# FFT mixer with two MLPs on one core: conversion slots, the centring of w1b, the start of the transforms and the banks of the transposes moved

## The chip, the core and the metric

The kernel runs on one core of a Trainium2 chip. The metric is the device time of one execution in microseconds (us). Work is spread over TensorE (PE, matmuls and transposes), VectorE (DVE), ScalarE (ACT), GpSimd (POOL) and the queue of SyncE (SP), which issues most DMAs. Each engine works through its own instructions in order, and semaphores make it wait for the others.

## What is computed

For four sequences of 3136 tokens with 256 channels, in float32:

```python
y = irfft(rfft(x, axis=1) * (filt_r + 1j * filt_i), n=3136)     # per channel
u = y + (y.transpose(0, 2, 1) @ U @ V).transpose(0, 2, 1)       # U 3136x32, V 32x3136
x2 = u + relu(u @ w1) @ w2                                      # 256 -> 1024 -> 256
xn = (x2 - mean(x2)) / sqrt(var(x2) + 1e-6) * g                 # over the channels
out = x2 + relu(xn @ w1b) @ w2b                                 # 256 -> 1024 -> 256
```

U, V and the four weights arrive as 64-bit floats.

## The kernel before

**Precision.** A float32 operand is split into a high and a low half (`hh`/`hl`, `ah`/`al`, `w1h`/`w1l` ...), and a product is made of three matmuls (high by high, high by low, low by high) at the fast rate.

**Main loop.** The 12544 tokens are cut into 25 blocks of 512. Phase ("a", k) is the first MLP of block k, ("b", k) the second. A phase has eight steps, one for each 128 of the 1024 hidden columns f. Step idx issues the first-layer matmuls of its f (`m1`, L671, into a bank `psh` from the pool `ps_h` of three), and the second-layer matmuls of the step two before (`m2`, L690 to L699, into `pso` from the pool `ps_o` of four). ACT makes `hh` from `psh`, then DVE makes `hl`. The steps begin with a0 f 0 to 3, a1 f 0 to 3, a0 f 4 to 7, a1 f 4 to 7 (steps 0 to 15), then a2 (16 to 23), b0, b1, a3, b2, a4, b3, a5 (from step 72). So the `m2` of a0 with f = 6 stands in step 12, and b0 begins in step 24. `end` closes a phase: for an a phase it spreads residual sums, halves and transposes on DVE over the steps behind it, for a b phase it scales and stores the output (`x2t`, L733).

**Units.** 28 units of 448 tokens hold the result of the inverse transform's last stage. `load_unit` loads `wt` of a unit from `bd` in DRAM (SP, L634), `unit` makes `ah` and `al` from it (PE, L642 and L644). Seven units make a batch, and unit 7 is the first of batch 1. It can only be loaded once the transform of batch 1 has ended with `tk` (`tstk`), and it is emitted in step 75 (f = 3 of a5, which looks ahead to block 6 by `ahead`).

**Transforms.** Batch 0 is transformed by `First` ahead of the main loop, batches 1 to 3 by the generator `fft` beside it. In each main step after `FFT0` a credit grows by `RATE` (by 0.4 once batch 1 is done), and each whole credit pulls the generator once. A batch takes 36 pulls: 1 for the first loads, 15 for stage one (L200 to L202 and `ze`), 2 empty, 17 for stage two, the filter and the way back (`be`, stored to `bd`), 1 for `tk`.

**First.** `rows` (eight rows, j = 0 to 7) does stage one of batch 0: PE multiplies `x` by `c` into `pz` (L450), DVE and ACT copy one half each to `big`. `c` is spread from a table of half size by two DVE operations (`spread`, L413), two rows ahead. `columns` (17 steps j) does the rest: PE turns a piece of `big` into `psz` (L538, bank "t", the only one of its pool), ACT copies it to `z`, PE transforms `z` (`ps2`, L555), ACT crosses it over (`psx`) and DVE and POOL apply the filter (`ya`, `xs`; `hl`, `hh` on odd turns; L228 to L232). Three steps later PE transforms back (`ps3`, L564, two banks of `ps_o`). In the step after that the "spill" copies it to `big` again (ACT for dh = 0, DVE for dh = 1), and DVE adds up the projection (`d`, L526 and L528).

**Conversions.** A weight is converted from 64 bits by a job of `to32`: ACT starts it with two operations (L808, L809), four word operations on DVE follow (L795 to L801), POOL multiplies and adds (L813, L815), `keep` makes the high half and `last` the low half. `stagger` runs 18 jobs; each `next(pr)` is one slot. Job i starts in slot 4 i, makes one word operation in each of the next four slots, is kept in slot 4 i + 8 and ends in slot 4 i + 9. The rows take slots 0 to 11 (`ROWSLOTS`), the columns one slot in each of steps 0 to 11 (`COLSLOTS`, slots 12 to 23), and each main step takes two, so step idx has slots 24 + 2 idx and 25 + 2 idx. Job 9 makes `w2h` and `w2l` for f = 6, 7; jobs 10, 11, 13 and 14 make `w1b`. Both jobs of one half of `w1b` are scaled by g (`wg`, L876), and behind the second one `after` is filled with the steps of the centring, one for each slot: `less` (PE sums the columns with four matmuls, L895, and DVE subtracts, L897), `high` (ACT), `low` twice (POOL, L904). `u_parts` (step 10) puts one more operation on POOL, `uh_sb` (L491).

**Order.** The program is recorded in the order in which it is written (`tc.manual_schedule`), and each engine keeps that order. A tile of a pool waits until the tile that had its buffer was read for the last time.

Of the kernel before, what the change touches and what calls it, by code (L numbers as in the profile page):

```python
# [10 lines left out]
F32 = mybir.dt.float32  # L11
# [3 lines left out]
AF = mybir.ActivationFunctionType  # L15
ALU = mybir.AluOpType
# [3 lines left out]
NB, N, D, R, FF = 4, 3136, 256, 32, 1024  # L20
P = 128
PP, NM, NG = 112, 28, 28
# [15 lines left out]
SLOTS, UAHEAD = 8, 2  # L38
PACE = 4
ROWSLOTS = (1, 2, 2, 2, 3, 3, 3, 4, 5, 5, 6, 6)  # L40
COLSLOTS = tuple(range(12))
VSTEP = 11
DIRECT = 4

PARTS, UPARTS = (0, 1, 2, 5, 6, 8), 10
LEAD = 3
FFT0, RATE = 25, 0.75

XTURN, XREAD, XSTAT, XROOT = (3, 4), 8, (10, 11), 12
BW = 32  # L50
# [90 lines left out]
def fft_mixer_kernel(ctx: ExitStack, tc: tile.TileContext, x, U, V, flt, w1, w2, gln, w1b, w2b,  # L141
                     c_fwd32, c_d32, c_e32, c_fwd, c_inv, c_e, c_d, c_w, out):
    nc = tc.nc
# [6 lines left out]
    ps_o = ctx.enter_context(tc.tile_pool(name="ps_o", bufs=4, space=PSUM))  # L150
    ps_t = ctx.enter_context(tc.tile_pool(name="ps_t", bufs=1, space=PSUM))
# [15 lines left out]
    def acopy(o, i, scale=1.0):  # L167
        nc.scalar.activation(out=o, in_=i, func=AF.Copy, scale=scale)  # L168
# [26 lines left out]
    def wide(dt, tag, name, w, bufs=2):  # L195
        t = fp.tile([PP, 2 * (D + R)], dt, tag=tag, name=name, bufs=bufs)
        return t[:, :2 * w].rearrange("p (a d) -> p a d", a=2)
# [6 lines left out]
    def flat(t):  # L204
        return t.rearrange("p a d -> p (a d)")
# [166 lines left out]
    class First:  # L372
# [36 lines left out]
        def spread(self, j):  # L409

            if j < NM // 4:
                for i in range(2):
                    nc.vector.tensor_scalar(out=self.c[j][:, :, i::2], in0=self.half[j // 2][:, j % 2 * 4:j % 2 * 4 + 4],  # L413
                                            scalar1=w_sb[:PP, 2 + i:3 + i], scalar2=None, op0=ALU.mult)

        def u32(self):
            hs, ls, ts = ([fp.tile([P, 512], F32, tag=tag, name=f"u{tag}", bufs=2)[:PP, :448] for j in range(2)]
# [82 lines left out]
        def columns(self):  # L500


            sp = Spectrum(0, self.flt)
            zt, n, w = {}, NCH, PP + R
            d0, d1 = self.d
            self.t = d1[:, 1, 0:KT * 2 * R].rearrange("p (h g r) -> p h g r", h=KT, g=2)
            turns = [self.u_half(h) for h in (1, 0)]

            def slot(g):
                return d1[:, 0] if g == 0 else d0[:, g % SLOTS]  # L510

            def total(j):
                if ADDL <= j < n + ADDL:
                    cross = sp.y[n - 1 - j + ADDL][1]
                    if cross:
                        cross()

            def spill(pvs, i):
                for dh, pv in enumerate(pvs):
                    (nc.vector.tensor_copy if dh else acopy)(self.big[:, dh, 2 * i * PP:2 * (i + 1) * PP].rearrange("p (g w) -> p g w", w=PP), pv[:, :, :PP])  # L520

            def project(pvs, i):
                for dh, pv in enumerate(pvs):
                    acc = self.t[:, dh]
                    if i == n - 1:
                        nc.vector.tensor_copy(acc, pv[:, :, PP:])  # L526
                    else:
                        nc.vector.tensor_tensor(out=acc, in0=pv[:, :, PP:], in1=acc, op=ALU.add)  # L528

            due = None  # L530
            for j in range(n + BACKL):
                if j < n:
                    i = n - 1 - j
                    ps = ps_t.tile([P, 512], F32, tag="t", name="psz")
                    for g in range(2):
                        for dh in range(KT):
                            a = g * D + dh * P
                            nc.tensor.transpose(ps[:PP, a:a + P], self.big[:, dh, (2 * i + g) * PP:(2 * i + g + 1) * PP], ident)  # L538
                total(j)
                if due:  # L540
                    spill(*due)
                    project(*due)
                due = None
                if j < n:
                    zt[i] = wide(F32, "fin", "z0", D, 3)
                    acopy(flat(zt[i]), ps[:PP])
                if 0 < j <= n:
                    i = n - j
                    z = zt.pop(i)
                    ps = ps_h.tile([P, 512], F32, tag="h", name="ps2")  # L550
                    if i == 0:
                        for g in range(2):
                            nc.tensor.matmul(ps[:, g * D:(g + 1) * D], self.e[:, 1 - g], z[:, g], start=True, stop=True)
                    else:
                        nc.tensor.matmul(ps, self.e[:, 0], flat(z), start=True, stop=True)  # L555
                    sp.filt(i, ps, True)
                if j >= BACKL:
                    i = n + BACKL - 1 - j
                    ya = sp.y.pop(i)[0]
                    pvs = []  # L560
                    for dh in range(KT):
                        ps = ps_o.tile([P, 512], F32, tag="o", name="ps3")
                        for g in range(2):
                            nc.tensor.matmul(ps[:, g * w:(g + 1) * w], dealt(ya[:, g], dh), slot(2 * i + g),  # L564
                                             start=True, stop=True)
                        pvs.append(ps[:, :2 * w].rearrange("p (g w) -> p g w", w=w))
                    due = pvs, i
                if j in UTURN:
                    next(turns[UTURN.index(j) // 2], None)
                self.filters(j + AHEAD)  # L570
                if BACKL - UAHEAD <= j < n + BACKL - UAHEAD:
                    i = n + BACKL - UAHEAD - 1 - j
                    for g in () if i else range(2):
                        acopy(slot(g)[:, PP:w], self.uf[:, g])
                    if i:
                        g = 2 * i % SLOTS
                        acopy(d0[:, g:g + 2, PP:w], self.uf[:, 2 * i:2 * i + 2])
                yield j
            project(*due)
            spill(*due)  # L580
# [273 lines left out]
    def w_job(nm, src, j, tag="flt"):  # L854
# [33 lines left out]
        def center():  # L888
            both = held.pop((nm, h))
            tiles = [[w[:, k, h * 512:(h + 1) * 512] for w in wts[nm]] for k in range(KT)]  # L890

            def less():
                ps = ps_h.tile([P, 512], F32, tag="h", name="psw")
                for k in range(KT):
                    nc.tensor.matmul(ps, ones, both[k], start=k == 0, stop=k == KT - 1)  # L895
                for k in range(KT):
                    nc.vector.tensor_tensor(out=both[k], in0=both[k], in1=ps, op=ALU.subtract)  # L897

            def high():
                for k in range(KT):  # L900
                    acopy(tiles[k][0], both[k])

            def low(k):
                aside.tensor_tensor(out=tiles[k][1], in0=both[k], in1=f32(tiles[k][0]), op=ALU.subtract)  # L904

            return [less, high, lambda: low(0), lambda: low(1)]

        return lambda: load64(tag, *rows), keep, last

# [168 lines left out]
```

## Time and profile before

| | us |
|---|---|
| median of 3 runs | 1390.94 |
| lowest and highest run | 1387.38, 1391.12 |
| profiled execution | 1388.34 |
| span of the profiled execution | 1386.6 |
| PE busy in the span | 1348.6 |
| DVE, ACT, POOL busy | 822.7, 550.8, 165.7 |

The profile is of one execution. Its span runs from the first to the last instruction. The rows give the start and the length of an instruction in us, the engine, the line, the operation, what it writes and reads, and in brackets how long the engine stood idle ahead of it and what it waited for. Durations of neighbours overlap a little, since instructions are pipelined; starts show the pace. The rows 0 to 33 us are `rows`, the columns run to 81 us, and the first matmul of the main loop starts at 88.75 us.

### The profile page before, as it was taken

What the parts mean: (1) busy time and instruction counts of PE and PEld (TensorE: products, weight loads), DVE (VectorE), ACT (ScalarE), POOL (GpSimd) and SP (SyncE); (2) the same over time, 40 slices, a digit from 0 to 9 for tenths busy, and PEclk for the clock granted to TensorE, in tenths of its full rate; (3) what the DMA queues carried; (4) which work ended last, traced back from release to release, by engine and by line L of the source; (5) the groups of instructions that cost most, each with busy time, mean ns of one, the idle gap of its engine ahead of it and who ended that gap; (6) DMA issues with size and microseconds to landing.
All of it is one profiled execution on the core that took longest, in us unless ns stands there. A gap on an engine that the chain in (4) does not pass through costs nothing.

```text
span 1386.6 us, 18686 instructions
## 1 busy us (share of the span) xinstructions
PE 1348.6 (97%) x6870; PEld 1123.5 (81%) x6870; DVE 822.7 (59%) x1660; ACT 550.8 (40%) x1034; POOL 165.7 (12%) x158
## 2 busy tenths in 40 slices
PE   8899999999899999999999999999999999999998
PEld 7577688877788888887888888878888888888887
DVE  6677975477455546666555546666545445545454
ACT  4755443466333324554333334554322222222221
POOL 2636430012000001111000001111000000000000
PEclk9999999999999999999999999999999999999999
DMA  9634357465525534444245344442122113200111
GB/s 258 238 96 136 91 134 197 126 194 164 142 72 146 140 78 138 136 132 118 68 126 142 99 125 138 135 150 74 43 62 65 31 36 83 65 16 31 46 47 39
DMA packets 140155, 151.10 MB, mean 109 GB/s; under 512 B 60528, under 2 KB 116160, under 8 KB 139968
## 3 DMA queue, kind: packets, MB, share of 16 engines
q1 hardware_dynamic: 133600, 138.61, 35.5%
q0 software_dynamic: 5888, 10.50, 3.2%
q8 instruction: 54, 0.88, 0.3%
q10 hardware_dynamic: 576, 0.80, 0.2%
q14 instruction: 37, 0.30, 0.1%
HBM read 102.34 MB, written 47.54 MB: 108 GB/s over the span
## 4 chain that ended last, share of the span: by engine, by line
PE 83%; DVE 7%; DMA 3%; ACT 3%; issue 2%; POOL 1%; SPq 1%; ACTq 0%; DVEq 0%; POOLq 0%
PE psh L671 35%; PE pso L698 12%; PE pso L699 6%; PE pso L690 6%; PE pso L692 6%; PE pso L691 6%; PE psu L642 3%; PE ps L200 2%; PE ps L202 2%; PE ps L201 2%; DMA x2t<-xd 2%; DVE x2t L733 1%; ACT xs L168 1%; PE psu L644 1%; DVE hl L675 1%
## 5 line engine op out<-in xcount | busy, mean ns | idle before, releaser
L675 DVE SCALAR_TENSOR_TENSOR hl<-psh,hh 128x512 fp32r<-128x512 f32 (+1 forms) x400 | 270.9, 678 | 411.1 <-ACT hh L674 410.8
L674 ACT ACTIVATE hh<-psh 128x512 fp32r<-128x512 f32 (+1 forms) x400 | 235.3, 588 | 628.7 <-PE psh L671 624.2
L698 PE MATMUL pso<-wb,hh 128*128 128x512 f32 x784 | 285.0, 397 | 1.8 <-DVE x L713 1.1
L671 PE MATMUL psh<-ah,wb 128*128 128x512 f32 (+1 forms) x800 | 276.7, 387 | 0.0
L699 PE MATMUL pso<-wb,hl 128*128 128x256 f32 x784 | 219.8, 280 | 0.6 <-DVE hl L675 0.6
L671 PEld LDWEIGHTS psh<-ah,wb 128*128 128x128 f32 x800 | 149.7, 188 | 33.3
L698 PEld LDWEIGHTS pso<-wb,hh 128*128 128x128 f32 x784 | 147.3, 188 | 36.0 <-DVE x L713 2.9
L690 PE MATMUL pso<-hh,w2h 128*128 128x512 f32 (+1 forms) x400 | 157.7, 394 | 5.9 <-DVE x2t L733 5.8
L692 PE MATMUL pso<-hh,w2l 128*128 128x512 f32 (+1 forms) x400 | 155.7, 389 | 2.6 <-POOL w2l L886 2.4
L671 PE MATMUL psh<-ah,w1h 128*128 128x512 f32 (+1 forms) x400 | 156.5, 391 | 0.6 <-DVE hl L675 0.4
L691 PE MATMUL pso<-hl,w2h 128*128 128x512 f32 (+1 forms) x400 | 155.5, 389 | 1.0 <-DVE hl L675 1.0
L671 PE MATMUL psh<-al,w1h 128*128 128x512 f32 (+1 forms) x400 | 155.7, 389 | 0.0
L671 PE MATMUL psh<-al,wb 128*128 128x512 f32 (+1 forms) x400 | 155.3, 388 | 0.0
L671 PE MATMUL psh<-ah,w1l 128*128 128x512 f32 (+1 forms) x400 | 155.0, 387 | 0.0
L699 PEld LDWEIGHTS pso<-wb,hl 128*128 128x128 f32 x784 | 148.0, 189 | 7.0 <-DVE hl L675 1.3
L236 POOL TENSOR_TENSOR xs<-xs,ft 128x512 f32<-128x512 f32 x42 | 54.3, 1293 | 392.0 <-ACT xs L168 392.0
L690 PEld LDWEIGHTS pso<-hh,w2h 128*128 128x128 f32 x400 | 75.6, 189 | 25.5 <-issue 8.7
L692 PEld LDWEIGHTS pso<-hh,w2l 128*128 128x128 f32 x400 | 75.7, 189 | 19.4 <-POOL w2l L886 3.9
L671 PEld LDWEIGHTS psh<-ah,w1h 128*128 128x128 f32 x400 | 75.8, 190 | 17.6 <-DVE hl L675 1.3
L671 PEld LDWEIGHTS psh<-ah,w1l 128*128 128x128 f32 x400 | 75.6, 189 | 16.0
L691 PEld LDWEIGHTS pso<-hl,w2h 128*128 128x128 f32 x400 | 75.7, 189 | 15.4 <-DVE hl L675 1.5
L671 PEld LDWEIGHTS psh<-al,w1h 128*128 128x128 f32 x400 | 75.8, 189 | 12.8 <-DVE al L171 0.4
(162 smaller groups left out, 1776.6 us busy)
## 6 DMA issues: line engine op xcount, KB each, us to landing
ft<-flt SPq DMA_DIRECT2D x42, 512.0 KB, 4.5
xd<-x SPq DMA_DIRECT2D x96, 128.0 KB, 2.9
x2t<-xd SPq DMA_DIRECT2D x24, 512.0 KB, 4.7
wt<-bd SPq DMA_DIRECT2D x24, 448.0 KB, 6.0
out<-x2t SPq DMA_DIRECT2D x84, 128.0 KB, 2.1
xt<-x SPq DMA_DIRECT2D x42, 224.0 KB, 4.2
zd<-ze SPq DMA_DIRECT2D x42, 224.0 KB, 2.9
zt<-zd SPq DMA_DIRECT2D x42, 224.0 KB, 3.2
```

Of the source, the lines that this page charges most:

```text
L200: nc.tensor.matmul(o, lh, rh, start=True, stop=False)
L201: nc.tensor.matmul(o, lh, rl, start=False, stop=False)
L236: nc.gpsimd.tensor_tensor(out=xs, in0=xs, in1=ft[:, :, 1], op=ALU.mult)
L642: nc.tensor.matmul(ps[:, m:UN:UW], t[:, m, dh * P:(dh + 1) * P], ic[:, m, :], start=m == 0, stop=False, skip_group_check=True)
L671: nc.tensor.matmul(ps[:, :n], w[:, kt, fs], a[:, kt, :n], start=j == 0, stop=j == 3 * KT - 1)
L674: nc.scalar.activation(out=hh[:, :n], in_=ps[:, :n], func=AF.Relu)
L675: nc.vector.scalar_tensor_tensor(out=hl[:, :n], in0=ps[:, :n], scalar=0.0, in1=f32(hh[:, :n]), op0=ALU.max, op1=ALU.subtract)
L690: nc.tensor.matmul(o, wh[:, f, ds], hh[:, :n], start=f == 0, stop=False)
L691: nc.tensor.matmul(o, wh[:, f, ds], hl[:, :n], start=False, stop=False)
L692: nc.tensor.matmul(o, wl[:, f, ds], hh[:, :n], start=False, stop=f == FT - 1)
L698: nc.tensor.matmul(o, hh[:, cs], w, start=f == 0, stop=False, skip_group_check=True)
L699: nc.tensor.matmul(o[:, D:], hl[:, cs], w[:, :D], start=False, stop=f == FT - 1, skip_group_check=True)
```

## The change

Five things are changed.

- `COLSLOTS` gives two slots to each of the columns' steps 0 to 2 and one to each of the steps 3 to 12: 16 in place of 12. The main loop then begins with slot 28.
- The centring has two empty slots ahead of `less`.
- `FFT0` is 24 and `RATE` 0.85: step 25 is the first to earn credit.
- The second half of `spread` is on ACT.
- In the columns `psz` takes a bank of `ps_o` in odd steps, and the copy to `z` is written ahead of the filter's sum and the spill.

```diff
-COLSLOTS = tuple(range(12))
+COLSLOTS = (0, 0, 1, 1, 2, 2) + tuple(range(3, 13))
...
-FFT0, RATE = 25, 0.75
+FFT0, RATE = 24, 0.85
...
             if j < NM // 4:
-                for i in range(2):
-                    nc.vector.tensor_scalar(out=self.c[j][:, :, i::2], in0=self.half[j // 2][:, j % 2 * 4:j % 2 * 4 + 4],
-                                            scalar1=w_sb[:PP, 2 + i:3 + i], scalar2=None, op0=ALU.mult)
+                src = self.half[j // 2][:, j % 2 * 4:j % 2 * 4 + 4]
+                nc.vector.tensor_scalar(out=self.c[j][:, :, 0::2], in0=src, scalar1=w_sb[:PP, 2:3], scalar2=None, op0=ALU.mult)
+                nc.scalar.activation(out=self.c[j][:, :, 1::2], in_=src, func=AF.Copy, scale=w_sb[:PP, 3:4])
...
-                    ps = ps_t.tile([P, 512], F32, tag="t", name="psz")
+                    ps = (ps_o if j % 2 else ps_t).tile([P, 512], F32, tag="o" if j % 2 else "t", name="psz")
...
+                    zt[i] = wide(F32, "fin", "z0", D, 3)
+                    acopy(flat(zt[i]), ps[:PP])
                 total(j)
...
-                if j < n:
-                    zt[i] = wide(F32, "fin", "z0", D, 3)
-                    acopy(flat(zt[i]), ps[:PP])
...
-            return [less, high, lambda: low(0), lambda: low(1)]
+            return [lambda: None, lambda: None, less, high, lambda: low(0), lambda: low(1)]
```

What this does to the order shows on three queues. First ACT in the columns around slot 16, which is `vh`, two DMAs to `vd` and the two operations that start a job (`cyh`, `cyl`); `z` is the copy of `psz`, `big` from `ps` the spill, `d` a copy for the back transform. Before, from step 3 on:

```order
L168 ACTIVATE big<-ps_517 128x224
L168 ACTIVATE z_543<-psz 112x512
L168 ACTIVATE psx<-ps_545 64x512 x2
L168 ACTIVATE d_184<-uf 128x2x32
L168 ACTIVATE vh<-ct 128x392
L916 DMA vd<-vh 128x392 x2
L808 ACTIVATE cyh<-stg 128x512
L809 ACTIVATE cyl<-stg 128x512
L168 ACTIVATE big<-ps_553 128x224
L168 ACTIVATE z_585<-psz 112x512
```

After, from step 2 on:

```order
L168 ACTIVATE vh<-ct 128x392
L915 DMA vd<-vh 128x392 x2
L807 ACTIVATE cyh<-stg 128x512
L808 ACTIVATE cyl<-stg 128x512
L168 ACTIVATE z_523<-psz 112x512
L168 ACTIVATE psx<-ps_527 64x512 x2
L168 ACTIVATE d_184<-uf 128x2x32
L168 ACTIVATE z_556<-psz 112x512
L168 ACTIVATE big<-ps_535 128x224
L168 ACTIVATE psx<-ps_564 64x512 x2
```

The work of slot 16 stands two steps sooner, and `z` stands ahead of the spill of its step. The same work of slot 20 moves from step 8 to step 5, and slot 24 comes into step 9.

Second POOL around `uh_sb`, in the main loop's steps 8 to 10. Before:

```order
L813 TENSOR_TENSOR cyl<-cyl,cyh 128x512
L1010 DMA e_sb<-c_e 112x512
L1011 DMA d_sb<-c_d 128x448
L886 TENSOR_TENSOR w2l<-ct,w2h 128x512
L815 TENSOR_TENSOR ct<-ct,cyl 128x512
L813 TENSOR_TENSOR cyl<-cyl,cyh 128x512
L491 TENSOR_TENSOR uh_sb<-uf,uh_sb 128x28x32
L886 TENSOR_TENSOR w2l<-ct,w2h 128x512
L815 TENSOR_TENSOR ct<-ct,cyl 128x512
```

After:

```order
L812 TENSOR_TENSOR cyl<-cyl,cyh 128x512
L1009 DMA e_sb<-c_e 112x512
L1010 DMA d_sb<-c_d 128x448
L885 TENSOR_TENSOR w2l<-ct,w2h 128x512
L814 TENSOR_TENSOR ct<-ct,cyl 128x512
L812 TENSOR_TENSOR cyl<-cyl,cyh 128x512
L491 TENSOR_TENSOR uh_sb<-uf,uh_sb 128x28x32
L814 TENSOR_TENSOR ct<-ct,cyl 128x512
```

The last `w2l` (f = 6, 7) stood behind `uh_sb` and now stands ahead of it, where the `w2l` of f = 4, 5 stood before.

Third SP around the load of unit 7, the first `wt` from `bd1`; `out` are the stores of phase b3, `xd4` and `x2t` belong to block 4, `xt` are the first loads of the next transform. Before:

```order
L271 DMA bd1_116<-be_3574 112x2x256
L751 DMA xd4_94<-x2_3409 32x16x64 x4
L271 DMA bd1_116<-be_3635 112x2x256
L271 DMA bd1_116<-be_3665 112x2x256
L743 DMA out<-x2t_3030 32x4x256 x4
L628 DMA ic_3726<-c_inv 112x448
L634 DMA wt_3725<-bd1_116 112x1024
L757 DMA x2t_3729<-xd4_94 128x4x256
```

After:

```order
L271 DMA bd1_116<-be_3535 112x2x256
L627 DMA ic_3591<-c_inv 112x448
L633 DMA wt_3590<-bd1_116 112x1024
L297 DMA xt_3615<-x 112x512
L297 DMA xt_3617<-x 112x512
L750 DMA xd4_94<-x2_3513 32x16x64 x4
L297 DMA xt_3670<-x 112x512
L742 DMA out<-x2t_3166 32x4x256 x4
```

The load stood behind the stores of block 4 and of phase b3, and now stands ahead of both.

## Rows read from the trace of the kernel before

**Rows 1.** The page's head: the span, and busy time of each engine.

```profile
span 1386.6 us, 18686 instructions
PE 1348.6 (97%) x6870; PEld 1123.5 (81%) x6870; DVE 822.7 (59%) x1660; ACT 550.8 (40%) x1034; POOL 165.7 (12%) x158
```

**Rows 2.** PE's waits over the span: line, releaser, total us, times, longest.

```profile
PE pso L690 <- DVE x2t L733: 5.8, 5, 1.3
PE psz L538 <- ACT z L168: 4.1, 4, 1.6
PE psu L642 <- DMA wt<-bd: 3.3, 1, 3.3
PE pso L692 <- POOL w2l L886: 2.4, 1, 2.4
PE psw L895 <- DVE hl L675: 1.9, 1, 1.9
PE psw L895 <- DVE wg L876: 1.3, 1, 1.3
...
PE pz L450 <- DVE c L413: 1.8, 2, 1.3
```

**Rows 3.** Stretches: length, busy PE, PEld, DVE, ACT, POOL, clock, DMA, GB/s.

```profile
130.00:135.00 5.00, 2.56 (x8) 1.72 (x7) 4.39 (x5) 1.46 (x3) 4.78 (x3) 0.80 0.13 39
135.00:140.00 5.00, 5.00 (x20) 4.07 (x19) 3.01 (x7) 1.10 (x2) 2.70 (x2) 0.85 0.28 98
...
160.00:165.00 5.00, 2.13 (x7) 0.71 (x5) 5.00 (x8) 3.43 (x6) 1.84 (x2) 0.88 0.70 154
165.00:170.00 5.00, 4.61 (x9) 3.02 (x10) 4.71 (x10) 1.23 (x2) 4.11 (x3) 0.50 0.63 215
...
375.00:380.00 5.00, 5.00 (x23) 4.51 (x23) 1.25 (x2) 1.16 (x3) 0.00 (x0) 0.66 0.95 254
```

**Rows 4.** Timeline: the main loop's first matmuls, then around unit 7.

```profile
88.75 0.40 PE L671 MATMUL psh<-ah,w1h 128*128 128x512 f32 x1
88.99 0.39 PE L671 MATMUL psh<-al,w1h 128*128 128x512 f32 x1
...
364.43 0.88 ACT L168 ACTIVATE tk<-tt 32x256 fp32r<-32x256 f32 x2 [0.68 <-DVE tt L278]
...
370.11 0.39 SPq L634 DMA_DIRECT2D wt<-bd  x1
...
374.39 1.16 PE L642 MATMUL psu<-ic,wt 112*128 112x112 f32 x8 [3.31 <-DMA wt<-bd]
```

**Rows 5.** Timeline of DVE and POOL in the main loop's steps 9 to 15.

```profile
123.04 3.40 DVE L797 TENSOR_SCALAR ct<-cyh 128x512 int32<-128x512 int32 x1
...
128.02 0.42 DVE L795 TENSOR_SCALAR cyh<-cyh 128x512 f32<-128x512 f32 x1
...
131.61 1.48 POOL L886 TENSOR_TENSOR w2l<-ct,w2h 128x512 fp32r<-128x512 f32 x1
...
142.26 1.92 POOL L813 TENSOR_TENSOR cyl<-cyl,cyh 128x512 f32<-128x512 f32 x1 [3.76 <-DVE cyh L801]
```

**Rows 6.** Timeline of DVE in the rows: one spreading of `c`, two operations.

```profile
18.66 0.58 DVE L413 TENSOR_SCALAR c<-cc,w_sb 112x224 f32<-112x224 f32 x2
```

**Rows 7.** Timeline of PE and ACT in the columns, steps 3 to 9.

```profile
40.90 1.10 PE L538 MATMUL psz<-ident,big 128*112 128x128 f32 x4 [0.89 <-ACT z L168]
...
48.54 0.52 ACT L168 ACTIVATE vh<-ct 128x392 fp32r<-128x392 f32 x1
...
51.52 0.59 ACT L168 ACTIVATE z<-psz 112x512 f32<-112x512 f32 x1
52.17 0.65 PE L538 MATMUL psz<-ident,big 128*112 128x128 f32 x4 [1.55 <-ACT z L168]
...
57.46 0.60 PE L538 MATMUL psz<-ident,big 128*112 128x128 f32 x4
...
59.74 0.60 PE L538 MATMUL psz<-ident,big 128*112 128x128 f32 x4
```

## The prediction

> **What bounds the kernel now.** I read the summary first. The span is 1386.6 us and TensorE (PE) is busy in 1348.6 us of it [rows 1]: 38 us of idle time, and what a lower clock costs, is all that a reordering can win, since the change removes no matmul. Second the list of PE's waits, which says where those 38 us lie: the largest single wait is 3.3 us on the load of `wt`, then 2.4 us on `w2l`, 1.9 and 1.3 us at the centring of `w1b`, and in the columns 4.1 us on the copy of `z`, in four pieces [rows 2]. The largest total, 5.8 us on `x2t`, is at the ends of the b phases, which the change does not touch. Third the table of stretches, for the clock: in these five the granted clock lies below 1, and each holds one of those waits or stands just behind one [rows 3]. The two levels are 2.4 and 1.2 GHz, so a stretch of 5 us at 0.80 lost 1.0 us. By this the stall on `w2l` lost 1.0 + 0.75 us more, the one at 160 us 0.6 + 2.5 us, the one on `wt` 1.7 us.
>
> **Part 1, the transform starts one step earlier and runs at 0.85.** Before, step 26 is the first to earn credit; the transform of batch 1 needs 36 pulls (1 + 15 + 2 + 17 + 1 in the code), which is 48 steps at 0.75, so it ends in step 73. Unit 7, the first of batch 1, is due in step 75. The trace agrees: `tk` is written at 364.4, SyncE issues the load at 370.1, behind the stores of a b phase, and PE stands 3.31 us until 374.4 [rows 4]. After, 36 pulls at 0.85 are 43 steps from step 25 on, so it ends in step 67 and the load is issued in step 68, seven steps ahead of its use. From `tk` to PE's start there lie 10 us [rows 4]; seven steps are some 20 us (an estimate: twelve matmuls a step that start 0.24 us apart [rows 4], so 2.9 us each). The wait goes, and its clock with it: 3.3 + 1.7 = **-5.0 us** (bounds -5.3 and -3.5: PE may meet a short wait on `x2t` in its place). The transform's matmuls only move. More pulls per step load VectorE (DVE) and ScalarE (ACT) more, but none of the waits that lead the list stands at a line of the transform [rows 2], so I cost that at nothing; where that cover is gone it is a few tenths of a us per pull.
>
> **Part 2, the conversions run ahead by four slots.** Slots 24 to 27 leave the main loop for the columns, and each later one runs two steps sooner. The job that makes `w2l` for f = 6, 7 ends in step 8 instead of 10, with its use in step 12. In the trace it stood behind `uh_sb` on GpSimd (POOL) and started at 131.61 [rows 5]; now it stands ahead of that. Two steps are more than 2.4 us, so this stall goes: -2.4 - 1.75 = -4.2 us gross. Next late is DVE. At 160 us it is busy for 5.00 of 5.00 us while PE has 2.13 [rows 3], and PE's 1.9 us there is a wait for `hl`, not for a conversion. During the stall on `w2l` DVE could catch up: it idled 0.6 us of the stretch from 130 and 2.0 us of the one from 135 [rows 3]. That time it no longer gets, so I take 2.5 us as given back at the later stall.
>
> **Part 3, two empty slots ahead of the centring.** `less` now comes two steps after `wg` is written instead of one, and by the slots still one step sooner than before. PE's 1.3 us on `wg` [rows 2] goes. Its four matmuls and its two DVE subtractions remain. New is that `low` lies one step ahead of the next `wg`, which takes its buffers, instead of two: DVE may wait there for a POOL operation, with the `hl` of that step queued behind and PE waiting for that. I cost it at nothing, as POOL waits for DVE rather than the reverse (3.76 us ahead of 142.26), and at one operation (1.48 us) if not [rows 5]. Parts 2 and 3 net: -4.2 - 1.3 + 2.5 = **-3.0 us**, bounds +1 (all given back, and `low` late) and -8 (the clock at 165 won as well).
>
> **Part 4, the rows.** The second half of `c` moves from DVE to ACT. Two halves take DVE 0.58 us [rows 6], and at two places PE waited for them, 1.8 us together [rows 2]; 0.29 us at each is saved: **-0.6 us** (0 to -0.9). ACT waits for PE's `pz` there, so its seven new operations hide; uncovered they are some 0.3 us each.
>
> **Part 5, the columns.** A step is 2.28 us where nothing waits (57.46 to 59.74), but steps 3 to 8 took 59.74 - 40.90 = 18.8 us, 3.14 each [rows 7]. The difference is ACT above all: in slot 16 it makes `vh`, issues two DMAs and starts a job, 2.98 us from 48.54 to the next `z` at 51.52, and PE's `psz` waits 1.55 us for it [rows 7]. With two banks `psz` no longer waits for the copy one step back, and `z` no longer stands behind the spill; but `ps2` still needs `z`, so only `psz` itself (0.60) and the spill are hidden from such a stall. Slot 16 also moves to step 2, behind which PE ran at half clock anyway (`psz` 1.10 against 0.60 us) [rows 7], which may hide most of its 1.55 us. Against it: one more slot with ACT work (at most the 2.98 us), four DVE word operations (0.42 us [rows 5]) and three POOL operations more; and `psz` of an odd step, in a bank of the `ps3` pool, now waits for DVE's accumulation from two steps back. Bounds: -3.5 (most of the 4.1 us on `z` gone) and +2.5 (the added ACT work unhidden, less the hidden `psz`). I take a small gain, nearest to the 1.55 us of the row at 52.17: **-1.2 us**.
>
> Open in this part are collisions of DVE and POOL: a word operation of 0.42 us took 3.40 us while POOL worked through its queue [rows 5]. The Trainium skill (SBUF — State Buffer, "SBUF: two separate sides") states that DVE and GpSimd share a pair of ports as an exclusive lock, so that the loser is blocked altogether. By that rule the three added POOL operations speak against this part; the row agrees, and the second rival follows it.
>
> **The sum.** -5.0 - 3.0 - 0.6 - 1.2 = -9.8 us. The profiled execution took 1388.34 us, 1.7 us of it around its span, so 1378.5 on its terms. It lies 2.6 below the median of 1390.94 and 1.1 below the mean of all four times; I add 1.0: **1379.5 us**.
>
> **Rivals.** (1) *DVE keeps the bill.* From 140 to 170 us DVE is the limit, and all that parts 2 and 3 free comes back as waits for `hl`; the columns come out even. For it: the stretch from 160. Against it: the conversions end two steps sooner. -5.0 - 0.6 gives 1383.7, with the same 1.0. (2) *Collisions.* With denser slots DVE stands behind POOL in the columns once or twice more, each 3.40 - 0.42 = 3 us, say 4.5, and parts 2 and 3 win nothing: -5.6 + 4.5 = -1.1, 1388.2. Against it: POOL is busy in 12% of the span [rows 1]. (3) *Everything opens.* Columns -4.0, parts 2 and 3 -6.5, as DVE meets POOL less often: -16.1, 1373.2. (4) *The start does not decide.* The load of unit 7 waits for something else than the transform, and the 5.0 us stay: 1384.5. Against it: `tk` is there 6 us before the issue [rows 4]. (5) *Slower, by the clock.* With three double slots first, PE stands in steps 1 to 3 long enough to fall to 1.2 GHz, and short waits in each step keep it there for ten steps. A step of 2.28 us then takes 4.56, against 3.14 now: +14.2 in place of -1.2, +5.6 in all, 1394.9. It decides once more than seven steps run low (7 x 1.42 us against the 8.6 us of the other parts and 1.6 to the median). For it: the clock did fall at 40.9. Against it: it was back later in the columns, and the 1.55 us wait did not bring it down (`psz` took 0.65 there) [rows 7].
>
> For the fifth the Trainium skill (TensorE: Matmul & The Clock Gate, "A second HAM failure mode: psum-queue depth-cycling") tells of a kernel that cycled through PSUM banks and idled briefly so often that its clock swung between the levels. The columns do cycle through banks with short waits, yet the rows show one fall in them, so this adds little to its chance.
>
> **How the numbers follow.** Forecast 0.48, DVE keeps the bill 0.20, collisions 0.12, everything opens 0.12, the start does not decide 0.03, clock 0.05. About 0.3%, 4.2 us, is what a measurement of this kernel can tell from no change: faster is below 1386.8, slower above 1395.1. Faster: 0.46 + 0.18 + 0.12 + 0.02 = 0.78. Slower, 0.05: the upper half of the fifth and the far ends of the second and the first. Same: 0.17. The range goes from 1372.5, just below the third, to 1387.0, above the first and the fourth; outside lie the fifth, more than half of the second and a part of the third, under 0.2 together. The bounds of the parts (+1 and -8, +2.5 and -3.5) ask for about the same width.
>
> **What would show it.** In the profile after: no PE wait on `wt` from `bd` and a clock of 1 near step 75 (part 1); no wait on `w2l` and none on `wg`, with smaller gaps of DVE ahead of 145 us and a wait for `hl` near 160 still there, which is the test against rival 1 (parts 2 and 3); the first main step some 2 us ahead of 88.75 [rows 4] (parts 4 and 5). A first main step later than that would put me wrong on the columns, waits on `hl` of over 5 us would put the first rival ahead, and a clock far below 1 throughout the columns the fifth.

## The result and the profile after

The changed kernel takes **1376.67 us** in the median of 4 runs (1375.45 to 1379.18), against 1389.89 (1387.38 to 1391.12) of the kernel before: ratio 0.9910, 95% interval 0.9887 to 0.9932, or -13.2 us. 1379.5 was predicted, with -10 against the mean of before. The profiled execution took 1375.62 us with a span of 1373.9. In the changed kernel the lines behind `spread` keep their place, and from L538 on those of the main loop are one lower than before (`x2t` L732, `hl` L674, `wg` L875, the centring's matmuls L894).

The head of the page and the longest waits of PE after, as in [rows 1] and [rows 2]:

```profile
span 1373.9 us, 18693 instructions
PE 1341.5 (98%) x6870; PEld 1118.7 (81%) x6870; DVE 823.4 (60%) x1653; ACT 554.0 (40%) x1041; POOL 165.6 (12%) x158
```

```profile
PE psz L538 <- DVE d L528: 3.2, 3, 2.1
PE pso L690 <- DVE hl L674: 3.1, 5, 1.0
PE pso L689 <- DVE x2t L732: 2.4, 2, 1.3
PE pso L697 <- DVE x L712: 2.3, 2, 1.2
...
PE psw L894 <- DVE hl L674: 1.6, 1, 1.6
...
PE psh L670 <- DVE hl L674: 1.4, 1, 1.4
PE ps L200 <- ACT be L168: 1.2, 3, 0.9
...
PE pz L450 <- ACT c L414: 0.7, 1, 0.7
```

The waits on `wt`, `w2l`, `wg` and `z` are gone. In the columns PE now waits for `d`, in the main loop for `hl`: for DVE at both places.

PE's idle time fell from 38.0 to 32.4 us (span less busy), its busy time from 1348.6 to 1341.5 us with the same 6870 instructions. So 7.1 of the 12.7 us by which the span is shorter are matmuls that ran at the higher clock or overlapped better, and 5.6 are waits.

Where it went shows when the span is cut at three starts of PE: the first `psz` (end of the rows), the first `psh<-ah,w1h` (end of the columns), and the first `psh<-ah,wb` (b0; by then most conversions are done). In us, one profiled execution each:

| kernel | rows | columns | conversion stage | from b0 on | span |
|---|---|---|---|---|---|
| before | 33.58 | 55.17 | 86.91 | 1210.94 | 1386.6 |
| the kernel before again (a1) | 31.20 | 53.91 | 85.80 | 1211.19 | 1382.1 |
| transform only (a2) | 32.81 | 54.94 | 87.40 | 1202.65 | 1377.8 |
| slots only (a3) | 32.87 | 55.72 | 80.95 | 1213.66 | 1383.2 |
| spread only (a4) | 31.34 | 53.91 | 87.40 | 1210.25 | 1382.9 |
| **after** | 31.13 | 57.09 | 81.28 | 1204.40 | 1373.9 |
| after, old transposes (b1) | 32.23 | 55.69 | 81.27 | 1204.21 | 1373.4 |
| after, copy late (b2) | 38.72 | 57.11 | 81.30 | 1204.27 | 1381.4 |
| after, one bank (b3) | 33.29 | 55.71 | 81.30 | 1204.30 | 1374.6 |
| after, no empty slots (c1) | 32.32 | 57.12 | 80.99 | 1203.57 | 1374.0 |
| after, pulls held (f1) | 32.66 | 57.14 | 81.31 | 1201.69 | 1372.8 |
| f1 and three more edits (e1) | 32.04 | 55.72 | 80.46 | 1201.48 | 1369.7 |
| after, less DVE (d1) | 33.18 | 57.09 | 77.85 | 1203.78 | 1371.9 |
| after, less POOL (d2) | 32.95 | 57.08 | 75.44 | 1201.53 | 1367.0 |

The rows differ by 2.4 us between two executions of the same code (before and a1), the columns and the conversion stage by about 1.2 us there; with a2 and a4, which leave these two stages as they were, the conversion stage spans 85.80 to 87.40. Among the versions of the changed kernel the last three columns repeat within 0.1 to 0.3 us where nothing was edited in them. So a stage tells what the median of whole runs cannot.

### The profile page after: what moved, and what is told of

It is laid out like the page before. It is cut to its first block, busy times and chain, and to the rows that moved or that the text cites. A ratio compares the mean times of both kernels' runs of the same rounds, so it can differ in the third digit from the quotient of the medians.

```text
span 1373.9 us, 18693 instructions
## 1 busy us (share of the span) xinstructions
PE 1341.5 (98%) x6870; PEld 1118.7 (81%) x6870; DVE 823.4 (60%) x1653; ACT 554.0 (40%) x1041; POOL 165.6 (12%) x158
## 4 chain that ended last, share of the span: by engine, by line
PE 84%; DVE 7%; ACT 3%; DMA 2%; issue 2%; POOL 0%; SPq 0%; ACTq 0%; DVEq 0%; POOLq 0%
PE psh L670 36%; PE pso L697 13%; PE pso L698 6%; PE pso L689 6%; PE pso L690 6%; PE pso L691 6%; PE psu L641 3%; PE ps L200 2%; PE ps L202 2%; PE ps L201 2%; ACT xs L168 1%; PE psu L643 1%; DVE x2t L732 1%; DVE hl L674 1%; DMA vd<-vh 1%
## 5 line engine op out<-in xcount | busy, mean ns | idle before, releaser
L674 DVE SCALAR_TENSOR_TENSOR hl<-psh,hh 128x512 fp32r<-128x512 f32 (+1 forms) x400 | 271.0, 678 | 412.2 <-ACT hh L673 411.8
L691 PEld LDWEIGHTS pso<-hh,w2l 128*128 128x128 f32 x400 | 75.1, 188 | 15.2
```

The lines of the kernel that those rows point to most:

```text
L674: nc.vector.scalar_tensor_tensor(out=hl[:, :n], in0=ps[:, :n], scalar=0.0, in1=f32(hh[:, :n]), op0=ALU.max, op1=ALU.subtract)
L691: nc.tensor.matmul(o, wl[:, f, ds], hh[:, :n], start=False, stop=f == FT - 1)
```

## Experiments: each part alone

The kernel before again, and one part of the change put into it at a time, all on one chip.

**a1, the kernel before, no edit.**

> The kernel before, profiled a second time. In the changed kernel the first transpose of the columns (psz) started at 31.13 us, 2.45 us sooner than before (33.58), where 0.6 was forecast. Theory chance: the first x arrives and PE runs the first row at another speed from one execution to the next (3.73 us for the 16 matmuls before, 2.01 after), so here too psz may start near 32 us. Theory spread: the start belongs to the kernel, psz at 33.4 to 33.7 again. The stalls on w2l (2.4 us), wt from bd (3.3 us) and the fall of the clock at 165 us should be there again, within 0.5 us each.

It took 1387.47 us, ratio 0.9992 (0.9975 to 1.0010). That is the noise of the method. The first `psz` came at 31.20, so the 31.13 of the changed kernel needs no cause in the change. The wait on `wt` was 4.1 us, 0.8 more than before, where within 0.5 was expected; the fall of the clock behind 160 us is there again. The trace holds a surprise: the wait on `w2l` is there, 2.44 us at 129.50 as before at 133.14, but the clock did not fall. The stretches of 5 us, columns as in [rows 3], of a1 around that wait:

```profile
125.00:130.00 5.00, 2.56 (x12) 1.81 (x11) 4.28 (x4) 1.92 (x4) 5.00 (x4) 1.00 0.27 94
130.00:135.00 5.00, 5.00 (x24) 4.08 (x23) 3.92 (x9) 1.42 (x3) 3.99 (x3) 1.00 0.38 105
```

In [rows 3] the two stretches have 0.80 and 0.85. a2 and a4 below run the same code there, with the same wait, and their clock fell, in a2 in two stretches (the second at 0.88), in a4 in one:

```profile
130.00:135.00 5.00, 2.85 (x8) 2.28 (x9) 4.37 (x6) 1.35 (x2) 4.06 (x4) 0.78 0.24 63
```

```profile
130.00:135.00 5.00, 5.00 (x16) 3.96 (x15) 2.41 (x6) 1.29 (x2) 3.99 (x3) 0.66 0.32 105
```

The same wait cost about 1.7 us of clock in three executions (1.75 before) and nothing in the fourth.

**a2, the transform alone.**

```diff
-FFT0, RATE = 25, 0.75
+FFT0, RATE = 24, 0.85
```

> The kernel before with FFT0 24 and RATE 0.85 alone. My theory: the wait on wt from bd and its clock go and nothing comes in their place: 5.0 us faster, -4.5 to -5.5, with all stages up to step 24 as before. Rival (the denser pulls give it back): DVE and ACT fall behind in steps 25 to 67, PE's waits at lines 200 to 202 and 642 grow by 2 us or more and the gain is 3 us or less.

1378.47 us against 1388.11, ratio 0.9930 (0.9903 to 0.9957): -9.6 us, and -8.3 us in the stage from b0 on. Both the theory (-4.5 to -5.5) and its rival (-3 or less) missed this. PE's waits from 180 us to the end in a2:

```profile
PE pso L690 <- DVE x2t L733: 2.4, 2, 1.3
PE pso L698 <- DVE x L713: 2.2, 2, 1.2
PE ps L200 <- ACT be L168: 1.2, 3, 0.9
PE psu L642 <- ACT be L168: 0.7, 3, 0.3
```

The wait on `wt` is gone, and of the 5.8 us on `x2t` [rows 2] 3.4 are gone too. What `x` and `be` take is some 2.5 us more than before.

**a3, the slots alone.**

```diff
-COLSLOTS = tuple(range(12))
+COLSLOTS = (0, 0, 1, 1, 2, 2) + tuple(range(3, 13))
```

> The kernel before with the new COLSLOTS alone. My theory: the columns become longer by 1 to 2.5 us (the added ACT and POOL work is not hidden there), the stall on w2l with its clock goes (-4.2), the waits at the centring stay (wg 1.3, and hl 1.9 or more): -1 to -3 in all. Rival (DVE keeps the bill): what w2l frees comes back as waits for hl between 140 and 175 us, and the total is 0 to +2.

This kernel has the sixteen slots but not the empty slots ahead of the centring. 1384.84 against 1388.11, ratio 0.9970 (0.9952 to 0.9988): -3.3 us. The conversion stage is 5 to 6 us shorter than in before and a1, at a clock of 1.00 where these have 0.94 and 0.96; the columns are 0.5 to 1.8 us longer. PE's waits in the conversion stage are now 1.07 and 2.46 us on `wg`, then 1.18 us on `hl`; none is left on `w2l`. Against this stands the stage from b0 on, 2.5 to 3.4 us longer than in before, a1 and a4, which have the same code there. Some 1.7 us of that are the clock behind the wait on `wt`: three stretches from 365 us on have 0.92, 0.50 and 0.89, 3.4 us lost against the 1.7 of before. And the transform's first matmul comes 17.5 us behind the start of b0 instead of 16.7.

**a4, the spread alone.**

```diff
-                for i in range(2):
-                    nc.vector.tensor_scalar(out=self.c[j][:, :, i::2], ...)
+                nc.vector.tensor_scalar(out=self.c[j][:, :, 0::2], in0=src, ...)
+                nc.scalar.activation(out=self.c[j][:, :, 1::2], in_=src, func=AF.Copy, scale=w_sb[:PP, 3:4])
```

> The kernel before with the second half of c on ACT alone. My theory: 0.6 us sooner at the first psz than the kernel before has in the same state of its first row, so 0 to -1 us in all, which is not to be seen in the total. Rival (the spread makes the whole of it): psz at 31.1 us, 2.4 us sooner than before, and 2 us in the total.

1387.64 us, ratio 0.9994 (0.9976 to 1.0012). Its rows take 31.34 us where a1, without the edit, has 31.20. Nothing can be seen of this part. The reason shows at the start of ACT, here in the changed kernel:

```profile
4.01 1.28 ACT L414 ACT_TABLE_LOAD   x1 [4.01 <-DMA cc<-c_fwd]
5.31 0.87 ACT L414 ACTIVATE c<-cc,w_sb 112x224 f32<-112x224 f32 x2
```

Before, ACT loaded its table at 0.74 us. Now its first instruction needs the table `cc`, the load stands behind that wait, and PE waits for `c` from ACT (0.7 us after, 1.2 us in a4). With 0.6 us for DVE's half a4 waits 1.8 us for `c`, as long as before; a1, without the edit, waits 0.4.

## Experiments: the transposes and the centring

Four versions of the changed kernel on one chip, each with something taken back; the kernel before took 1387.42 us there.

**b1, old transposes.**

```diff
-                    ps = (ps_o if j % 2 else ps_t).tile(...)
-                    zt[i] = wide(F32, "fin", "z0", D, 3)
-                    acopy(flat(zt[i]), ps[:PP])
+                    ps = ps_t.tile([P, 512], F32, tag="t", name="psz")
...
+                if j < n:      # behind the filter's sum and the spill
+                    zt[i] = wide(F32, "fin", "z0", D, 3)
+                    acopy(flat(zt[i]), ps[:PP])
```

> The changed kernel with the transposes of before: one bank for psz, the copy to z behind the spill. The columns (first psz to the main loop's first matmul) took 57.1 us in the changed kernel and 53.9 to 55.2 in the four profiles that have the old transposes and the old slots, 55.7 with the new slots alone. Theory banks cost: psz of an odd step waits for DVE's sums (3.2 us in the list of PE's waits), so without the two banks the columns take 54.5 to 55.9 and the total is 1 to 2.5 us less. Rival (the slots cost it): 57 us again, and the total the same.

1375.32 us, ratio 0.9918 (0.9903 to 0.9933), columns 55.69.

**b2, two banks with the copy late**: only the second half of b1's edit.

> The changed kernel with two banks for psz, but the copy to z behind the spill as before. Theory banks cost: 57 us or more in the columns, with psz waiting for DVE's d (about 3 us) and now for z as well. Rival (the early copy is what costs, since the spill and then DVE's sums come later by it): 55 to 56 us.

1378.58 us, ratio 0.9945 (0.9924 to 0.9965), columns 57.11. Its profiled execution lost 5 us and more in the rows: two waits for `c` of ACT took 4.4 us, and the granted clock was 0.82 over that stage (PE busy for 32.53 us, 26.70 in the changed kernel). ACT itself had stood 4.96 us for the table `cc` there, which DVE's half waited for too. The other runs were shorter.

**b3, one bank with the copy early**: only the first half.

> The changed kernel with one bank for psz, but the copy to z ahead of the spill. Theory banks cost: 54.5 to 55.9 us in the columns, no psz wait on d. Rival (the early copy costs): 57 us.

1376.51 us, ratio 0.9928 (0.9912 to 0.9945), columns 55.71.

So the early copy is worth nothing (57.09 and 57.11; 55.71 and 55.69), and the second bank **costs 1.4 us**. The timeline of the changed kernel around step 7 shows how, first DVE, ACT and its DMA issues, then PE:

```profile
50.09 0.52 ACT L168 ACTIVATE vh<-ct 128x392 fp32r<-128x392 f32 x1
50.63 1.08 ACTq L915 DMA_DIRECT2D vd<-vh  x2
51.76 0.67 ACT L807 ACTIVATE cyh<-stg 128x512 f32<-128x512 f32 x1 [1.16 <-issue]
...
53.37 0.35 ACT L168 ACTIVATE big<-ps 128x224 f32<-128x224 f32 x1
...
53.75 0.36 DVE L528 TENSOR_TENSOR d<-ps,d 128x64 f32<-128x64 f32 x2 [1.72 <-ACT big L168]
...
54.12 0.62 PE L538 MATMUL psz<-ident,big 128*112 128x128 f32 x4 [2.06 <-DVE d L528]
```

ACT is held by slot 20's `vh`, two DMAs and job start. The spill `big` stands behind these, DVE's sum `d` waits 1.72 us for the spill, and `psz` in a bank of `ps_o` waits 2.06 us for that sum. Before, `psz` in these steps waited only for ACT's `z`. In b1 the whole span has 2.3 us of waits on `z` for it, the longest 0.9:

```profile
PE psz L538 <- ACT z L168: 2.3, 4, 0.9
```

**c1, no empty slots ahead of the centring.**

```diff
-            return [lambda: None, lambda: None, less, high, lambda: low(0), lambda: low(1)]
+            return [less, high, lambda: low(0), lambda: low(1)]
```

> The changed kernel without the two empty slots ahead of the centring. From the first matmul of the main loop to the first of phase b0 the changed kernel takes 81.3 us, and the kernel with the new slots alone 80.95, with waits of PE on wg of 3.5 us. Theory DVE is the limit there: without the empty slots the wait on wg is back (2 to 4 us), the waits on hl are less by the same, and the stretch is 80.5 to 82. My forecast's theory: the empty slots are worth 1.3 us, so 82.5 or more.

1376.99 us, ratio 0.9938 (0.9916 to 0.9959). The conversion stage takes 80.99 us without them and 81.28 with them. PE's only listed wait in that stage in c1:

```profile
PE psw L894 <- DVE wg L875: 3.5, 2, 2.4
```

The changed kernel has 4.4 us there on `hl` instead (1.6, 1.4 and 1.4). The empty slots turn waits on one DVE result into waits on another; c1 pays 0.6 us of clock (busy PE 77.48 against 76.88) and waits less; a3, with the same two waits, kept a clock of 1.00. From b0 on c1 is 0.8 us shorter.

## Experiments: what limits the conversion stage

The two probes take work off one engine each in the conversions of the main loop (`thin` is a list that is empty until the main loop begins). In d1 the weights converted there lose their signs, in d2 their low words lose a correction. The stretch of the conversion stage: length, then busy time (instructions) of PE, PEld, DVE, ACT and POOL, PE's clock, DMA share, GB/s. Before, after, and the two probes:

```profile
88.75:175.66 86.91, 81.00 (x362) 64.06 (x360) 71.60 (x111) 44.12 (x81) 50.87 (x36) 0.94 0.37 106
```

```profile
88.22:169.50 81.28, 76.88 (x362) 61.49 (x360) 71.04 (x105) 42.95 (x79) 48.12 (x34) 1.00 0.37 105
```

```profile
90.27:168.12 77.85, 76.38 (x361) 61.64 (x360) 64.61 (x95) 42.91 (x79) 46.83 (x34) 1.00 0.39 110
```

```profile
90.03:165.47 75.44, 75.44 (x362) 61.88 (x361) 62.46 (x108) 42.58 (x79) 17.37 (x14) 1.00 0.43 119
```

**d1, one of DVE's four word operations less.**

```diff
-        nc.vector.scalar_tensor_tensor(out=tb, in0=s[:, :, 1], scalar=-0x80000000, in1=tb, ...)
+        if not thin:
+            nc.vector.scalar_tensor_tensor(out=tb, in0=s[:, :, 1], scalar=-0x80000000, in1=tb, ...)
```

> A probe of the conversion stage: the changed kernel with one of VectorE's operations left out of every conversion that runs in the main loop's first part, the one that puts the sign bit into the word (the weights converted there lose their signs). Theory: VectorE's own work is the limit of the conversion stage; then the stage shortens from 81.3 to 76 to 78 us, and the waits of the matmuls on hl and hh go. Rival: the collisions with GpSimd or the order of the steps is the limit; then it shortens by less than 1.5 us.

One execution: 77.85 us, 3.4 less, with 6.4 us less of DVE. Of the 4.4 us of waits on `hl` 1.4 are left.

**d2, POOL's multiplication and addition left out.**

```diff
-        nc.gpsimd.tensor_tensor(out=lf, in0=lf, in1=h, op=ALU.mult)
+        if not thin:
+            nc.gpsimd.tensor_tensor(out=lf, in0=lf, in1=h, op=ALU.mult)
...
+        if not thin:
+            nc.gpsimd.tensor_tensor(out=t, in0=t, in1=lf, op=ALU.add)
```

> A probe of the conversion stage: the changed kernel with GpSimd's multiplication and addition left out of every conversion that runs in the main loop's first part (the low words converted there lack their last correction). Theory of collisions: VectorE's operations are stretched while GpSimd works; without them the operations over 1 us in that stretch go, and the stage shortens from 81.3 by 4 us or more. Rival: VectorE's work itself is the limit; then its busy time in the stage falls little and the stage shortens by 1 us or less.

One execution: 75.44 us, 5.8 less, and PE waits for nothing (busy 75.44 of 75.44). DVE did everything that it does in the changed kernel (1653 instructions in the span of either) and yet was busy for 8.6 us less in this stage, 11.3 in the span. The groups of one word operation (line, shape, count | busy us, mean ns), after and then d2:

```profile
L796 DVE TENSOR_SCALAR ct<-cyh 128x512 int32<-128x512 int32 x11 | 12.1, 1098 | 0.0
```

```profile
L796 DVE TENSOR_SCALAR ct<-cyh 128x512 int32<-128x512 int32 x11 | 5.2, 477 | 0.0
```

This operation changed most. In the order L794, L796, L798, L800 the four word operations took 827, 1098, 947 and 415 ns in the mean in this stage, and 464, 477, 682 and 691 in d2: the last became longer, and one of them, 1.54 us at 106.25, ran beside a POOL operation that is left.

So DVE is the limit of this stage, as both probes show. A part of its time, 8.6 of 71.0 us by d2, is not work of its own but time stretched while POOL works. The Trainium skill (SBUF — State Buffer, "SBUF: two separate sides") states that the two share ports under an exclusive lock; d2 agrees, with 1098 against 477 ns for the same operation. That POOL's work itself was late is not excluded by d2; no wait of PE in the changed kernel names POOL in this stage, and DVE stood there for POOL's `ct` for 0.6 us.

## Experiments: the ends of phases, and a version with more

The waits on `x2t` that a2 took away were not in the prediction, so their cause was open. DVE in the changed kernel at the end of a b phase, and PE behind it:

```profile
512.22 0.69 DVE L674 SCALAR_TENSOR_TENSOR hl<-psh,hh 128x512 fp32r<-128x512 f32 x1 [1.82 <-ACT hh L673]
512.83 0.68 DVE L243 TENSOR_TENSOR ya<-ya,xs 128x512 f32<-128x512 f32 x1
513.43 0.69 DVE L171 TENSOR_TENSOR lo<-zt,hi 112x512 fp32r<-112x512 f32 x1
514.21 0.69 DVE L171 TENSOR_TENSOR yl<-ya,yh 128x512 fp32r<-128x512 f32 x1
515.43 0.69 DVE L228 TENSOR_TENSOR ya<-ps,ft 128x512 f32<-128x512 f32 x1 [0.53 <-ACT xs L168]
516.04 3.22 DVE L732 SCALAR_TENSOR_TENSOR x2t<-pso,ln,x2t 128x256 f32<-128x256 f32 x8
...
517.44 0.47 PE L689 MATMUL pso<-hh,w2h 128*128 128x512 f32 x1 [1.31 <-DVE x2t L732]
```

One pull of the transform's second stage puts four operations on DVE (3.2 us from 512.83 to 516.04) ahead of the eight that empty `pso`, and the next phase's first `m2` waits for its bank.

**f1, no pull in a step in which a phase has just ended.**

```diff
-                    if credit >= 1:
+                    if credit >= 1 and not (idx >= 2 and steps[idx - 2][1] == FT - 1):
```

> The changed kernel with one condition more: the transform is not advanced in a step of the main loop in which a phase of stage one has just ended, the credit being kept for the next step. Theory: the waits of about 1.3 us at the ends of phases (pso<-x2t 2.4 us, pso<-x on the line after it 2.3 us in the changed kernel) come from a stage-two step whose vector operations queue ahead of the eight copies of the phase's end. Then those two rows fall to under 1.2 us together, and the time from the first matmul of w2b's blocks to the end goes from 1204.4 to about 1201 us, 1373.5 in all. Rival: the phase's end waits for VectorE's other work there; then the rows stay at 2 us each and the stretch stays within 0.7 us of 1204.4.

1374.62 us against 1387.14, ratio 0.9908 (0.9892 to 0.9925). PE's waits from 200 us on in f1, the longest group first:

```profile
PE ps L200 <- ACT be L168: 2.9, 6, 0.9
PE ps L200 <- DVE ya L228: 0.9, 2, 0.4
PE pso L690 <- DVE hl L674: 0.7, 1, 0.7
```

No wait on `x2t` is left, one of the two on `x` is left (1.2 us), and the stage from b0 on falls by 2.7 us to 1201.69 (1201 was expected). 1.7 us come back on `be`: the pulls that were held now come denser. The cause of these waits is settled; as whole runs f1 and the changed kernel, which were not on one chip, can't be told apart.

**e1, three more edits on f1.** Old transposes as in b1, `wg` on ACT, ACT's share of the spread only from the third row on:

```diff
-                nc.vector.tensor_scalar(out=held[nm, h][kt], in0=t, scalar1=g_sb[:, kt:kt + 1], ...)
+                nc.scalar.activation(out=held[nm, h][kt], in_=t, func=AF.Copy, scale=g_sb[:, kt:kt + 1])
```

> The previous kernel's idea, with three changes of the first half beside it: all transposes of z in one bank and the copy late, as before the change; the scaling of w1b's four blocks by g on ScalarE instead of VectorE; ScalarE's share of the spread coefficients only from the third row on. Theory (VectorE is the limit of the conversion stage, two banks cost the columns their 1.4 us): columns 55.7 instead of 57.1, conversion stage 81.3 less the four operations of 0.38 us, about 79.8, and the rest 1201; in sum some 5 us under the changed kernel, 1370 to 1372 us. Rival (ScalarE, by its own queue in the conversion stage, holds the centring as much as VectorE did): the conversion stage stays at 81 or goes over 82, and the sum gains no more than 4 us.

1373.05 us (1371.08 to 1374.40), ratio 0.9893 (0.9876 to 0.9911), 14.1 us under the kernel before; 1370 to 1372 was expected. Columns 55.72 and the time from b0 on 1201.48 are as expected. The conversion stage is 80.46: four operations of 0.48 us less on DVE gave 0.8 us, between theory and rival. The stages behind the rows add up to 5.1 us under the changed kernel, the medians against their own runs of before only to 0.9 us. It is the fastest version tried of those that compute everything, but that it beats the changed kernel is shown by the stages, not by the intervals of whole runs, which overlap.

## Why the prediction came out as it did

The time lies in the range, 2.8 us under the forecast. The sum had the right sign, but two of its terms were too small and one had the wrong sign. Measured by the stages, before to after:

| part | predicted | measured |
|---|---|---|
| 1, transform | -5.0 | -8.3 alone (a2), -6.5 in the stage from b0 on with all parts |
| 2 and 3, slots and empty slots | -3.0 | -4.5 to -6.1 in the conversion stage, of which some 1.3 come back behind b0 |
| 4, rows | -0.6 | not to be told from 0 (a4) |
| 5, columns | -1.2 | +1.9 to +3.2 |
| sum | -9.8 | -12.7 (spans) |

That the sum came out near is in part luck. By these stages the one from b0 on is 1.5 us better than its term, the conversion stage 2.6 and the rows 1.8, which a1 has without any edit; the columns are 3.1 us worse. Part 5's miss hides most of what parts 1 to 3 were short.

**Part 1 was right in its mechanism and short in its cover.** The load of unit 7 was to be issued some 20 us ahead of its use. In the changed kernel SP and PE have:

```profile
342.58 0.30 SPq L633 DMA_DIRECT2D wt<-bd  x1
...
366.11 1.04 PE L641 MATMUL psu<-ic,wt 112*128 112x112 f32 x8
```

That is 23.5 us, and PE does not wait; the 3.3 us and the clock behind them are gone, which are the predicted 5.0. The step that failed is the sentence that the change does not touch the ends of the b phases. A pull is placed by the credit, and which pulls fall on the step of a phase's end changes with `FFT0` and `RATE`: five waits on `x2t` became two. "None of the waits that lead the list stands at a line of the transform" was true by the line of the waiting matmul and false by what was ahead of its releaser. The added pulls per step, costed at nothing, cost 1.4 us on `be`. `x` took 1.1 us more, at an end of a phase again (one of its two waits went in f1). The "few tenths of a us per pull" where cover is gone is shown by no row; the pull at 512.83 held DVE for 3.2 us and PE for 1.31. Of a2's 8.3 us, idle time is 5.5 and PE's busy time 2.8, of which 1.7 are the clock behind `wt`; the last 1.1 us have no row.

**Parts 2 and 3 were right on the bill and short on the clock.** 3.7 us of waits on `w2l` and `wg` went. The prediction gave 2.5 back as waits for `hl`; the rows show 4.4 after against 1.9 before, 2.5 more. The mis-sized term is the clock. The two stretches above show it: PE's idle time in the stage fell only from 5.9 to 4.4 us, its busy time from 81.00 to 76.88 us at the same 362 instructions, with a clock of 0.94 and 1.00. The clock gave 4.1 us, where 1.75 were in the sum and the 3.1 of 160 to 170 us stood only in the far bound. All four executions with the old slots (before, a1, a2, a4) had the fall behind 160 us, and none of the ten with the new slots had one of that size: only c1 had any in this stage. After, four stretches there read:

```profile
150.00:155.00 5.00, 3.56 (x15) 2.27 (x13) 5.00 (x9) 1.85 (x3) 1.50 (x2) 1.00 0.04 16
155.00:160.00 5.00, 3.37 (x10) 1.81 (x10) 5.00 (x7) 1.81 (x4) 2.88 (x2) 1.00 0.70 169
160.00:165.00 5.00, 4.76 (x21) 3.92 (x22) 5.00 (x10) 3.73 (x7) 1.01 (x1) 1.00 0.51 149
165.00:170.00 5.00, 4.36 (x20) 3.29 (x19) 5.00 (x6) 1.46 (x3) 4.92 (x4) 1.00 0.01 2
```

DVE is busy for 5.00 in each, as at 160 before, but PE's idle time is spread: at most 1.63 us in one stretch, against 2.87 before. Of the clock's gain the part behind `w2l` varies: three of four executions had that fall, and the one without it (a1) has a stage of 85.80, 1.1 to 1.6 us under the others. The empty slots themselves (part 3) are worth nothing (c1, a3): the step that failed is that PE's wait on `wg` goes with nothing in its place, since waits on `hl` of the same size came. With the conversions earlier and DVE no faster, 15.2 us pass from the start of b0 to the transform's first matmul in the changed kernel, 13.9 in a2: the 1.3 us that come back.

**Part 4** was 0.6 us on a stage that varies by 2.4, and the table load moved behind a wait was not seen ahead: all seven operations were taken as hidden behind PE's `pz`, and the first two (at 5.31) stand ahead of any `pz`. Each of the later ones takes 0.5 us on ACT, not 0.3 (0.50 at 12.12).

**Part 5 had the wrong sign**, inside its bounds (+2.5 from before, a little over it from a1). The prediction named both terms against it, the added ACT work and the wait of an odd step's `psz` for DVE's accumulation, and priced neither in the value it took. The first is 0.5 to 1.8 us (55.7 against 55.2 and 53.9 us; the clock over the columns was 0.97 in the first two and 1.00 in a1), the second 1.4 us (b1, b3). The step that failed is taking the value nearest to the 1.55 us wait on `z`: the wait was won, and a longer one on `d`, at the end of the same chain through ACT, took its place.

**The rivals.** The first (DVE keeps the whole bill) is refuted by the conversion stage, though its mechanism is real: it kept 2.5 us and the stage's remaining waits. The second (collisions) did not occur in the columns, where no word operation of DVE took over 1.03 us; d2 shows collisions in the conversion stage, and there the word operation at L796 (L797 before) took 1.10 us in the mean after and 1.09 before. The fourth and fifth did not occur either: `wt` is early, and in the columns one stretch (40 to 45 us) ran at 0.73 and the one ahead at 0.93, where before had 0.66 in one and a1 1.00. The main loop's first step came at 88.22, 0.5 us ahead of before [rows 4] instead of 2; the prediction named that as the test for parts 4 and 5, and the columns alone lost 1.9 us, and the 2.4 us that the rows gained are in a1 too, without any edit. The third (everything opens) came half true: the conversion stage gave most of its 6.5, though not by fewer meetings of DVE with POOL, and the columns none of their 4.0.

## What to carry to other kernels

Behind a wait, read what stood ahead of the releaser in its queue: the line of the waiting matmul told of a phase's end, and the cause was a transform that any change of rate shifts. When a buffer is given a second bank, look who empties that bank: a bank shared with a consumer further down the chain swaps a short wait for a longer one. In a stage where one engine is busy throughout, earlier starts only move the waits to another of its results; its own work, or what slows that work, must become less. And one execution does not tell what a wait costs in clock: look at several.

## What the runs showed of the hardware

- The same 2.4 us wait of PE was followed by a granted clock of 0.80 and 0.85 in two stretches in one execution, of 0.78 and 0.88 in a2, of 0.66 in a4, and of 1.00 throughout in a1, all with the same code there. In the changed kernel PE was idle for 6.3 us between 125 and 180 us, in seven waits of 1.6 us or less, at a clock of 1.00 throughout. The levels of the clock are 2.4 and 1.2 GHz; 1.00 is the higher one throughout a stretch.
- Leaving out 24 operations of GpSimd made VectorE's busy time fall by 11.3 us with the count of its instructions unchanged (d2).
- Two DMA issues on ScalarE's queue took 1.08 us, and its next operation started behind them (the row at 50.63). ScalarE's table load waits for the operands of the first operation behind it (4.01 against 0.74 us).
- The first stage (rows) takes 31.1 to 33.6 us with the same or nearly the same code, and 38.7 in one execution, so gains of under 2 us there need many runs.
